# Which heads the two softmax engines take, and twelve exp tiles in flight instead of eight

## The chip, the cores and the metric

The kernel runs on one core of one Trainium2 chip. Time is device time in microseconds. Before the change, four runs gave a median of 1343.49 us (1343.4 to 1343.71). One further look is the profiled execution, whose trace is read below.

A core has a matrix engine (TensorE, in the trace PE, its weight loads apart as PEld), a vector engine (VectorE, DVE), a scalar engine (ScalarE, ACT), a general engine (GpSimd, POOL) and a queue engine (SyncE, SP). Each works through its own list of instructions in order; semaphores tie the lists together.

## The reference

Two kinds of layer alternate, A, B, A, B, on x of shape 2048 x 512 in bf16. Cut to what matters:

```python
def A(x, w_r, w_i):                      # spectral
    X = rfft2(x); X = X * (w_r + 1j * w_i)
    return irfft2(X)

def B(x, wq, wk, wv, wo):                # 32 heads of 16, one shared K and V
    q = (x @ wq) split into heads; k = x @ wk; v = x @ wv
    p = softmax(q k^T / 4); return (p v, heads joined) @ wo

x = x + A(layernorm(x)); x = x + B(layernorm(x))
x = x + A(layernorm(x)); x = x + B(layernorm(x))
```

Both layers A share one filter, both layers B one set of weights.

## The kernel before, in words

**Layers.** A layer pair is A, then B. The spectral transform is done as matmuls with cosine and sine tables along both axes, with small additions and subtractions (radix steps) on DVE between them: a forward part (`add_front`), a middle with the second transform and the filter (`add_middle`), and a way back, layer norm and the K and V projections (`add_back`). Near the end of the filter, `radix_d` (L1177) makes sums and differences of the filtered spectrum with `radix2` (L56), four tiles of 4 x 512 called xd, which the inverse matmuls in `inv` (L1186) read.

**Attention.** There are 32 blocks in a layer: four blocks of 512 query columns, times eight sets of four heads. A block meets 16 chunks of 128 keys. One unit is one head of one block with one chunk: a score matmul (32 contraction rows, 128 keys, 512 queries), an exponential, and a matmul with V (PV) that also sums the denominator. The four heads of a block lie in the four 32-row strips of the matrix array: a score matmul of head h uses strip h, and score matmuls of different strips run side by side. PV matmuls use four 32-column strips, one per head, and are issued in packs of four.

**Two ways to exponentiate.** ACT takes two heads at once: two score matmuls fill one of two double PSUM buffers "sa", one exp (L1318) reads both and writes an SBUF tile "e". DVE takes one head: one score matmul fills one of four PSUM buffers "b"; a first phase (L1325, `p1`) makes the bits of a bf16 power of two by a multiply and an add, and two more phases are this pattern plus a constant, added on 64-bit words by POOL (L1329) or, rarely, by DVE (L1331). PV then reads three phases, with weights that make a smoother approximation.

**The planner.** No order is written by hand. When the program is built, `Plan` keeps an estimated clock per engine and, step by step, issues whichever candidate can start first (`run`, L197). `do_scores` (L478) issues a run of up to five score tiles: the kind (ACT or DVE) whose engine would run dry first. `peek` (L614) says which heads a kind would take next, and `take` (L628) takes them. The four heads of a chunk belong at first to one kind, and an idle kind may take the rest of the other's. ACT takes the first two in order; DVE takes the first one whose strip is not already used in the present run. If a strip repeats in a run, `do_scores` counts another pass. `usable` (L351) refuses another ACT score when as many exp tiles are unread by PV as `E_BUFS` (L131) allows, which is 8. `round` (L416) forms packs of four PV matmuls, and lets smaller ones go when a kind has reached its limit. `fill` (L454) inserts dummy matmuls on zeros where the planner sees too little matmul activity.

Around the attention the same planner issues the work of the neighbouring layers: query projections, output projections (L1366), statistics, the next layer's front part. The result is a fixed list for each engine.

**Buffers.** Thirteen tiles "e" of 128 x 1024 bf16 serve exp tiles and some short-lived tiles (`t2`, L981, takes the one that was freed longest ago; `free2`, L990, gives it back). `wrote` (L993) drops a write-after-write wait when the same engine wrote the buffer before.

Of the kernel before, what the change touches and what calls it, by code (L numbers as in the profile page):

```python
# [8 lines left out]
ACT = mybir.ActivationFunctionType  # L9
ALU = mybir.AluOpType  # L10
P = 128
BF = mybir.dt.bfloat16
# [40 lines left out]
    return tabs  # L53


def radix2(nc, sd, x, piece):  # L56

    nc.vector.tensor_tensor(out=sd[:, 2 * piece:2 * piece + 2, :], in0=x[:, 0:2, :], in1=x[:, 2:4, :],  # L58
                            op=ALU.subtract if piece else ALU.add)


def radix4(nc, sd, x, half, o, piece):
# [53 lines left out]
class Plan:  # L116
# [12 lines left out]
    PORT = True  # L129
    POOL_LAG = 2600.0  # L130
    E_BUFS = 8  # L131
    T_BUFS = 4
    WIN = 3413.0
    WARM = 3500.0
# [17 lines left out]
    def __init__(self):  # L152
        self.t = {"PE": 0.0, "ACT": 0.0, "DVE": 0.0, "POOL": 0.0}
        self.mode = ""
        self.sa = [0.0, 0.0]
        self.bank = [0.0] * self.NB
        self.use = [None] * self.NB
        self.bg = {"PE": [], "ACT": [], "DVE": [], "POOL": []}
        self.n = 0
        self.hist = []  # L160
        self.at = None
        self.act_fifo, self.p1_fifo, self.ph_fifo, self.pool = [], [], [], []
        self.pv = []
        self.half = None
        self.live = {"ACT": 0, "DVE": 0}
        self.bufs = {"ACT": self.E_BUFS, "DVE": self.T_BUFS}
        self.dve_last = ""
        self.acc_of = {}
        self.bg_last = self.port = 0.0
        self.ranks, self.base = None, 0  # L170

    def ranked(self, which):
# [24 lines left out]
    def run(self, goal):  # L197
        while not goal():
            best = None
            for c in (self.pe_next(), self.act_next(), self.dve_next(), self.pool_next()):  # L200
                if c is not None and (best is None or c[0] < best[0]):
                    best = c
            best[1](best[0], *best[2:])


# [210 lines left out]
    def round(self):  # L416
        at = self.at
        avail = []
        free = self.slot_free("b")
        for e in sorted(self.pv, key=lambda e: e[:2]):  # L420
            if (e[2] in self.acc_of or free is not None) and e[4] // 4 in at.v_ready:
                avail.append((max(e[0], at.v_ready[e[4] // 4]),) + e[1:])
        if not avail:
            return None
        b0 = min(e[2] for e in avail)
        t0 = 0.0 if b0 in self.acc_of else free
        heads, sel = set(), []
        for e in avail:
            if e[2] == b0 and e[3] not in heads:
                heads.add(e[3])  # L430
                sel.append((max(e[0], t0),) + e[1:])
        if len(sel) < 4 and b0 + 1 in self.acc_of:
            for e in avail:
                if e[2] == b0 + 1 and e[3] not in heads:
                    heads.add(e[3])
                    sel.append(e)
        full = any(self.live[k] >= self.bufs[k] for k in ("ACT", "DVE"))
        return sel if len(sel) == 4 or self.made(b0) or full else None

    def made(self, b, h=None):  # L440
# [147 lines left out]
class Attn:  # L588
# [25 lines left out]
    def peek(self, kind, strips=()):  # L614


        cur = self.cur[kind]
        if not cur and self.groups:
            b, kc = self.groups[0]
            cur = [(b, kc, h) for h in range(4)]  # L620
        if not cur:
            other = self.cur["DVE" if kind == "ACT" else "ACT"]
            cur = other if kind == "DVE" or len(other) > 1 else []
        if kind == "ACT":
            return cur[:2]
        return sorted(cur, key=lambda u: u[2] in strips)[:1]

    def take(self, kind, us):  # L628
        if not self.cur[kind] and self.groups:
# [48 lines left out]
class Layer:  # L678
# [83 lines left out]

    def add_middle(self):
        p, em = self.plan, self.em
        self.mid, self.fil = [], []
        for u in range(4):
            evs, two = [], u in self.two
# [21 lines left out]
            if u == 3 and not two:  # L789
                a = p.add("DVE", 1733.0, evs[:2], lambda k, u=u: em.filt(self, u, 0, 2), order=10 + u, port=True)  # L790
# [10 lines left out]
    def add_back(self):  # L801
        p, em, at = self.plan, self.em, self.at
        left = [T]
        for t in range(T):
            o = 20 + 10 * t
            cs = []
            for b in range(2):
                es = []
                for j in range(2):
                    if t == 0 and not self.direct:  # L810
# [3 lines left out]
                                  lambda k, t=t, b=b, j=j, m=m: em.inv(self, t, b, j, m.slot, (1,)), order=o)  # L814
                    elif t == 0:
# [3 lines left out]
                                  lambda k, b=b, j=j, m=m: em.inv0(self, b, j, m.slot, 1), order=o)  # L819
# [8 lines left out]
            for j in range(0, R, w):  # L828
                key, ks = ("b", t, j), []
                for i, r in enumerate(range(j, j + w)):  # L830
# [11 lines left out]
                    z = p.add("DVE", 597.0, [y], lambda k, t=t, r=r, y=y: em.add_x(t, r, y.slot), give=(y,), order=o + 1)  # L842
# [15 lines left out]
            def v_got(k, t=t):  # L858
                at.v_ready[t] = k.end + p.LAT[k.eng]
                left[0] -= 1  # L860
                if left[0] == self.EARLY:
                    at.dve_on = True
                    at.dve_from = k.end - 2000.0
# [61 lines left out]
class Emit:  # L925


    def __init__(self, ctx, tc, ins, out):
# [21 lines left out]
        self.part = const.tile([P, 2], F32, name="part")  # L950
        self.wv = const.tile([P, NC, DH], BF, name="wv")
        self.tc = tc
        self.e2 = [const.tile([P, 1024], BF, name=f"e2_{i}") for i in range(13)]
        self.idle, self.home, self.writer = list(range(13)), {}, {}
        self.WO = const.tile([P, 4, D], BF, name="WO")
        self.junk = const.tile([P, 512], BF, name="junk")
        self.eps = const.tile([P, 1], F32, name="eps")
# [197 lines left out]
    def turn(self, L, u, piece):  # L1155
        if piece == 0:
            L.sd_of[("x", u)] = self.t4([4, 512])
        radix2(self.nc, L.sd_of[("x", u)], L.X[u], piece)
        if piece:
            L.X[u] = L.sd_of.pop(("x", u))  # L1160

# [14 lines left out]

    def radix_d(self, L, u, piece):  # L1177
        if piece == 0:
            L.Dz[u] = self.t4([4, 512], tag="xd", bufs=4)
        radix2(self.nc, L.Dz[u], L.X[u], piece)  # L1180

    def load_it(self, L, t):
        L.IT[t] = self.t4([4, 640], tag="it", bufs=2)
# [2 lines left out]
    def inv(self, L, t, b, j, slot, ks):  # L1186
        for v in range(T):
            if v <= t + 1 and v not in L.IT:
                self.load_it(L, v)
        ps = self.ps(slot).rearrange("p (u x) -> p u x", u=2)  # L1190
        for k in ks:
            u = 2 * j + k
            for a in range(2):
                for i in range(2):
                    w = 128 * (3 - (t * a + i) % 4)
                    z = L.Dz[u][:, 2 * (t % 2) + a, 256 * i + 128 * b:256 * i + 128 * b + 128]
                    self.nc.tensor.matmul(ps[:, k, :], lhsT=z, rhs=L.IT[t][:, u, w:w + 256], start=(a == 0 and i == 0),  # L1197
                                          stop=(a == 1 and i == 1), skip_group_check=True)

    def inv0(self, L, b, j, slot, k):  # L1200

# [255 lines left out]
```

The softmax here doesn't subtract the row's maximum and nothing guards it: scores larger than these inputs give would overflow.

## Time and profile before

| what | value |
| --- | --- |
| median of four runs | 1343.49 us |
| profiled execution, its own time | 1343.71 us |
| profiled execution, span | 1341.9 us |
| score matmuls on PE | 4096 (L1313) |
| PV matmuls on PE | 7360: 2464 for exp tiles, 4896 for phases (L1335) |
| exps on ACT | 1232, mean 1094 ns |
| first phases on DVE | 1632, mean 675 ns |
| phase adds on POOL | 815, mean 1049 ns |
| sums and differences into xd on DVE | 16, median 683 ns (L58) |

The span runs from the first to the last instruction of the program. "Busy" is the time in which an engine shows an instruction. An instruction's shown duration can reach over the start of the next one on the same engine, so busy time is more than what the engine needs, and the step from one start to the next says more. A line such as "A <- B: 8.4, 8, 4.0" in the waits view says that A's engine stood idle for 8.4 us in 8 waits, 4.0 at most, until B released it. L numbers are lines of the kernel before.

### The profile page before, as it was taken

To read this page: it belongs to the slowest core of one execution; us is meant where nothing else is said; L and a number is where in the kernel's file an instruction comes from. 1 tells how busy PE (TensorE), PEld (TensorE's weight loads), DVE (VectorE), ACT (ScalarE), POOL (GpSimd) and SP (SyncE) were. 2 spreads that over 40 slices of the span, in tenths; PEclk is the share of its full clock that TensorE was granted. 3 is DMA by queue.
4 is the path that set the end of the run, shared out by engine and by line. 5 is a ranking of instruction groups with operands and counts; after the bars stand their busy time and mean duration, and the time that the engine had idled before them with its cause. 6 is when DMAs were issued, how large, how long until landed. Compare 5 with 4: busy or idle time off the path is not lost. (4 is left out here: it accounts for less than half of the span.)

```text
span 1341.9 us, 31571 instructions
## 1 busy us (share of the span) xinstructions
PE 1305.1 (97%) x12978; PEld 428.4 (32%) x13046; DVE 1291.2 (96%) x2317; ACT 1225.6 (91%) x1390; POOL 848.1 (63%) x831
## 2 busy tenths in 40 slices
PE   9999999999999999999999999999999999999998
PEld 5642223222222232222246422222222222322222
DVE  6998999999999999999969999999999999999998
ACT  6478999999999999899954889999999999998996
POOL 0004777767776777667720068777777777876775
PEclk9999999999999999999999999999999999999999
DMA  9100000010001000100051000000000000000000
GB/s 292 41 1 1 2 1 2 2 33 1 2 2 33 1 2 2 32 2 2 1 165 41 1 2 1 2 2 6 13 2 2 6 13 2 2 1 17 1 1 17
DMA packets 29041, 25.16 MB, mean 19 GB/s; under 512 B 8672, under 2 KB 27616, under 8 KB 28896
## 3 DMA queue, kind: packets, MB, share of 16 engines
q1 hardware_dynamic: 28608, 22.58, 5.8%
q8 instruction: 102, 1.67, 0.5%
q10 hardware_dynamic: 288, 0.56, 0.1%
q14 instruction: 43, 0.35, 0.1%
HBM read 17.89 MB, written 3.67 MB: 16 GB/s over the span
## 5 line engine op out<-in xcount | busy, mean ns | idle before, releaser
L1318 ACT ACTIVATE e<-sa 128x1024 bf16<-128x1024 f32 x1232 | 1142.6, 1094 | 24.6 <-PE sa L1313 20.1
L1329 POOL INT64_ADD w<-w x815 | 845.3, 1049 | 475.4 <-DVE w L1325 425.9
L1325 DVE TENSOR_SCALAR w<-b 128x512 uint16<-128x512 f32 x1632 | 996.1, 675 | 7.5 <-PE sa L1313 3.4
L1335 PE MATMUL b<-w,vs 128*32 128x512 bf16 x4896 | 544.3, 385 | 2.4 <-POOL w L1329 1.1
L1335 PE MATMUL b<-e,vs 128*32 128x512 bf16 x2464 | 411.5, 386 | 1.0 <-DVE w L1325 0.4
L1313 PE MATMUL sa<-w,KA 32*128 32x512 bf16 x1248 | 257.5, 381 | 6.1 <-ACT e L1318 3.8
L1313 PE MATMUL b<-w,KB 32*128 32x512 bf16 x832 | 255.5, 381 | 2.8 <-DVE w L1325 1.7
L1313 PE MATMUL sa<-w,KB 32*128 32x512 bf16 x1216 | 252.5, 381 | 5.6 <-ACT e L1318 2.2
L1335 PEld LDWEIGHTS <-vs 128*32 128x32 bf16 x7360 | 142.6, 94 | 330.7 <-issue 316.1
L1313 PE MATMUL b<-w,KA 32*128 32x512 bf16 x800 | 235.7, 381 | 0.7 <-DVE w L1325 0.2
L1313 PEld LDWEIGHTS <-KB 32*128 32x128 bf16 x2048 | 84.0, 91 | 224.0 <-issue 218.5
L1313 PEld LDWEIGHTS <-KA 32*128 32x128 bf16 x2048 | 82.3, 91 | 226.0 <-issue 217.9
L1342 DVE STREAM_TRANSPOSE raw<-b 128x512 f32<-128x512 f32 x64 | 44.8, 700 | 4.0 <-PE b L1335 4.0
L1028 DVE BATCH_NORM_STATS2 st<-x_sb 128x6 f32<-128x512 bf16 x52 | 35.3, 679 | 4.2 <-DMA x_sb<-in_A_x_dram 3.8
L1248 DVE TENSOR_TENSOR x_sb<-b,x_sb 128x512 bf16<-128x512 f32 x52 | 34.4, 675 | 3.4 <-PE b L1366 2.6
L1297 PE MATMUL b<-gx,wq 128*128 128x512 bf16 x101 | 35.2, 385 | 0.8 <-issue 0.2
L1366 PE MATMUL b<-WO,w 128*128 128x512 bf16 x116 | 34.2, 382 | 1.3 <-DVE w L1325 0.5
L1197 PE MATMUL b<-it,xd 128*128 128x256 bf16 x256 | 30.8, 273 | 3.2 <-DVE xd L58 3.2
L1237 PE MATMUL b<-tab_PS,w 128*128 128x512 bf16 x122 | 31.0, 379 | 0.5 <-issue 0.3
L1099 PE MATMUL b<-tab_PH,e 128*128 128x512 bf16 x118 | 30.5, 380 | 0.9 <-ACT w L1112 0.3
L1257 ACT CAST e<-b 128x512 bf16<-128x512 f32 x28 | 16.0, 587 | 15.4 <-PE b L1197 14.9
L1197 PEld LDWEIGHTS <-xd 128*128 128x128 bf16 x256 | 24.4, 98 | 9.5 <-DVE xd L58 3.9
(84 smaller groups left out, 572.8 us busy)
## 6 DMA issues: line engine op xcount, KB each, us to landing
it<-const_IT SPq DMA_DIRECT2D x8, 640.0 KB, 6.5
w<-const_FT SPq DMA_DIRECT2D x8, 512.0 KB, 7.1
x_sb<-in_A_x_dram SPq DMA_DIRECT2D x4, 512.0 KB, 6.9
w<-in_A_w_r_dram SPq DMA_DIRECT2D x8, 256.0 KB, 6.7
w<-in_A_w_i_dram SPq DMA_DIRECT2D x8, 256.0 KB, 7.1
out_dram<-x_sb SPq DMA_DIRECT2D x16, 128.0 KB, 1.8
way<-x_sb SPq DMA_DIRECT2D x6, 256.0 KB, 2.2
tab_PH<-const_PH ACTq DMA_DIRECT2D x1, 512.0 KB, 5.1
```

The lines of the kernel that those rows point to most:

```text
L1028: self.nc.vector.bn_stats(st, self.ps(slot) if slot else self.x[:, x[1], x[0], :])
L1197: self.nc.tensor.matmul(ps[:, k, :], lhsT=z, rhs=L.IT[t][:, u, w:w + 256], start=(a == 0 and i == 0), stop=(a == 1 and i == 1), skip_group ...
L1237: self.nc.tensor.matmul(self.ps(slot), lhsT=L.UT[t][:, b, r, 128 * i:128 * i + 128], rhs=self.PS[:, s, :], start=(s == 0), stop=(s == n - ...
L1248: self.nc.vector.tensor_tensor(out=x, in0=self.ps(slot), in1=x, op=ALU.add)
L1297: self.nc.tensor.matmul(self.ps(slot), lhsT=self.wq[:, c, g * 128:(g + 1) * 128], rhs=self.xTc(at, qb, c), start=(c == 0), stop=(c == NC - ...
L1313: self.nc.tensor.matmul(o, lhsT=KX[rs, kc * P:(kc + 1) * P], rhs=at.QT[qb][rs, g, :], start=True, stop=True, skip_group_check=True)
L1318: self.wrote("ACT", e, self.nc.scalar.activation(out=e, in_=self.ps(slot), func=ACT.Exp, scale=SCALE))
L1325: self.nc.vector.tensor_scalar(out=t[0][:, j], in0=self.ps(slot), scalar1=P1_SCALE, scalar2=P1_BIAS, op0=ALU.mult, op1=ALU.add)
L1329: self.nc.gpsimd.int64_add(t[p][:, 0:n].bitcast(U64), t[0][:, 0:n].bitcast(U64), DELTA[p] * FOUR)
L1335: self.nc.tensor.matmul(self.ps(slot)[32 * h:32 * h + 32, :], lhsT=V[:, kc, :], rhs=rhs, start=first, stop=last, skip_group_check=True)
L1342: self.nc.vector.transpose(out=at.raw[(qb, g)][:, par].rearrange("p a b -> p (a b)"), in_=self.ps(slot))
L1366: self.nc.tensor.matmul(self.ps(slot), lhsT=at.OT[t][:, g, r * P:(r + 1) * P], rhs=self.WO[:, g, :], start=(g == 0), stop=(g == g1 - 1), s ...
```

## The change

There are four parts.

1. `peek` sorts the heads that a kind may take. Heads whose strip is already used in the present run come last; for DVE this is the old rule, for ACT it is new. Among the rest, when the other kind has one or two heads left of its chunk, the heads in those strips come last.
2. The limit of unread exp tiles is 12 (`E_LATE`) instead of 8 from the moment the last V tile of a layer is ready until `add_middle` plans the next layer. Otherwise it stays 8.
3. The tiles xd are gone. `radix_d` writes the sums and the differences into one "e" tile each, eight in a layer; each is given back after its fourth use in `inv`. There are 21 tiles "e" instead of 13, in place of the four xd tiles, which are twice as large.
4. If nothing can be issued, `run` sets a flag under which `round` lets a smaller pack go, instead of failing.

```diff
-def radix2(nc, sd, x, piece):
+def radix2(nc, o, x, piece):
+    nc.vector.tensor_tensor(out=o, in0=x[:, 0:2, :], in1=x[:, 2:4, :], op=ALU.subtract if piece else ALU.add)
...
     E_BUFS = 8
+    E_LATE = 12
...
+            if best is None:
+                assert not self.force
+                self.force = True
+                continue
+            self.force = False
             best[1](best[0], *best[2:])
...
-        full = any(self.live[k] >= self.bufs[k] for k in ("ACT", "DVE"))
+        full = self.force or any(self.live[k] >= self.bufs[k] for k in ("ACT", "DVE"))
...
+        taken = lambda x: {u[2] for u in self.cur[x]} if 0 < len(self.cur[x]) <= 2 else ()
         if kind == "ACT":
-            return cur[:2]
-        return sorted(cur, key=lambda u: u[2] in strips)[:1]
+            d = taken("DVE")
+            return sorted(cur, key=lambda u: (u[2] in strips, u[2] in d))[:2]
+        a = taken("ACT")
+        return sorted(cur, key=lambda u: (u[2] in strips, u[2] in a))[:1]
...
     def add_middle(self):
+        p.bufs["ACT"] = p.E_BUFS
...
             def v_got(k, t=t):
                 left[0] -= 1
+                if left[0] == 0:
+                    p.bufs["ACT"] = p.E_LATE
...
-        self.e2 = [const.tile([P, 1024], BF, name=f"e2_{i}") for i in range(13)]
+        self.e2 = [const.tile([P, 1024], BF, name=f"e2_{i}") for i in range(21)]
...
     def radix_d(self, L, u, piece):
         if piece == 0:
-            L.Dz[u] = self.t4([4, 512], tag="xd", bufs=4)
-        radix2(self.nc, L.Dz[u], L.X[u], piece)
+            L.Dz[u] = [[self.t2([2, 512]), 4] for _ in range(2)]
+            for z, _ in L.Dz[u]:
+                self.writer.pop(self.home[id(z)][0], None)
+        radix2(self.nc, L.Dz[u][piece][0], L.X[u], piece)
...
     def inv(self, L, t, b, j, slot, ks):
-                    z = L.Dz[u][:, 2 * (t % 2) + a, 256 * i + 128 * b:256 * i + 128 * b + 128]
+                    z = L.Dz[u][t % 2][0][:, a, 256 * i + 128 * b:256 * i + 128 * b + 128]
+            d = L.Dz[u][t % 2]
+            d[1] -= 1
+            if d[1] == 0:
+                self.free2(d[0])
```

More of the change, by code (lines that the diff above doesn't have):

```diff
@@ L53, in host_tables @@
     return tabs
-def radix2(nc, sd, x, piece):
-    nc.vector.tensor_tensor(out=sd[:, 2 * piece:2 * piece + 2, :], in0=x[:, 0:2, :], in1=x[:, 2:4, :],
-                            op=ALU.subtract if piece else ALU.add)
+def radix2(nc, o, x, piece):
+    nc.vector.tensor_tensor(out=o, in0=x[:, 0:2, :], in1=x[:, 2:4, :], op=ALU.subtract if piece else ALU.add)
 def radix4(nc, sd, x, half, o, piece):
@@ L202, in run @@
                     best = c
+            if best is None:
+                assert not self.force
+                self.force = True
+                continue
+            self.force = False
             best[1](best[0], *best[2:])
@@ L952, in __init__ @@
         self.tc = tc
-        self.e2 = [const.tile([P, 1024], BF, name=f"e2_{i}") for i in range(13)]
-        self.idle, self.home, self.writer = list(range(13)), {}, {}
+        self.e2 = [const.tile([P, 1024], BF, name=f"e2_{i}") for i in range(21)]
+        self.idle, self.home, self.writer = list(range(21)), {}, {}
         self.WO = const.tile([P, 4, D], BF, name="WO")
@@ L1157, in turn @@
             L.sd_of[("x", u)] = self.t4([4, 512])
-        radix2(self.nc, L.sd_of[("x", u)], L.X[u], piece)
+        radix2(self.nc, L.sd_of[("x", u)][:, 2 * piece:2 * piece + 2, :], L.X[u], piece)
         if piece:
```

## The prediction

> **What bounds the kernel now.** I read the page first: busy shares, then its chain.
>
> ```profile
> span 1341.9 us, 31571 instructions
> PE 1305.1 (97%) x12978; PEld 428.4 (32%) x13046; DVE 1291.2 (96%) x2317; ACT 1225.6 (91%) x1390; POOL 848.1 (63%) x831
> ...
> PEclk9999999999999999999999999999999999999999
> ...
> ACT e L1318 19%; DVE w L1325 8%; PE b L1335 6%; PE sa L1313 3%; PE b L1313 3%; DVE w L1170 1%; DVE x_sb L1248 1%; DVE st L1028 1%; PE b L1366 1%; DVE raw L1342 0%; PE b L1297 0%; PE b L1197 0%; PE b L1237 0%; PE b L1010 0%; DVE xnt L1052 0%
> ```
>
> Three engines look full, the TensorE clock is full everywhere, and the chain hops between ACT, DVE and PE. DMA queues carry nothing here. So I cut the span where the DVE's first-phase line (L1325) starts and stops in each layer; the columns of this windows view are the length, then busy time and count of PE, PEld, DVE, ACT, POOL.
>
> ```profile
> 111.06:678.72 567.66, 557.12 (x5746) 158.69 (x5766) 562.60 (x962) 556.69 (x611) 418.48 (x410) 1.00 0.04 10
> 678.72:776.47 97.75, 92.02 (x711) 52.48 (x719) 79.95 (x196) 54.87 (x85) 2.48 (x3) 1.00 0.18 55
> 776.47:1331.50 555.03, 545.53 (x5732) 156.18 (x5749) 550.30 (x922) 544.91 (x590) 423.32 (x408) 1.00 0.01 4
> ```
>
> The two attention stages (call them B and D) are 1122.7 of 1341.9 us, and only they are touched. "Busy" flatters ACT: an exp shows 1097 ns, but in the chain view of stage D runs of exps follow each other faster, 106.64/116 = 0.919 us each:
>
> ```profile
> 947.83 42.58 ACT e L1318 x46
> 1104.03 106.64 ACT e L1318 x116
> ```
>
> Start to start, the commonest step is 0.904 us for an exp and 0.598 us for a DVE first phase. Summing, over the records, what each step is longer than that gives the true slack: ACT 23.1 us in B and 22.0 in D (means 0.942 and 0.941), DVE 11.9 and 8.7 (mean 0.606). DVE is the tightest engine, ACT next. Much of ACT's slack is a few holes, in the waits view of B and the same view of D, and the timeline shows the largest:
>
> ```profile
> ACT e L1318 <- PE sa L1313: 8.4, 8, 4.0
> ```
> ```profile
> ACT e L1318 <- PE sa L1313: 8.6, 6, 2.0
> ```
> ```profile
> 551.83 4.69 ACT L1318 ACTIVATE e<-sa 128x1024 bf16<-128x1024 f32 x5
> 560.55 1.94 ACT L1318 ACTIVATE e<-sa 128x1024 bf16<-128x1024 f32 x2 [4.03 <-PE sa L1313]
> ```
>
> In that hole PE runs the output projection (L1366) and hardly any PV matmuls (L1335), so exp tiles stay unread; at eight unread ones the planner may issue no more ACT scores.
>
> PE's score groups, last. A score matmul uses one of four 32-row strips, and a group is the run of score matmuls between other PE work:
>
> ```profile
> 525.94 0.38 PE L1313 MATMUL b<-w,KB 32*128 32x512 bf16 x1
> 525.95 0.60 PE L1313 MATMUL sa<-w,KB 32*128 32x512 bf16 x2
> 526.47 0.39 PE L1335 MATMUL b<-e,vs 128*32 128x512 bf16 x1
> ...
> 528.10 0.39 PE L1313 MATMUL sa<-w,KB 32*128 32x512 bf16 x2
> 528.11 0.39 PE L1313 MATMUL b<-w,KB 32*128 32x512 bf16 x1
> 528.42 0.40 PE L1335 MATMUL b<-w,vs 128*32 128x512 bf16 x3
> ```
>
> Both groups hold three score matmuls. In the first, DVE's head sits in the same strip as one of ACT's pair; the third matmul starts 0.22 us late and PV follows after 0.53 us. In the second all strips differ: 0.32 us. Over all groups the medians are 0.531 to 0.534 and 0.322: a repeated strip costs 0.21 us.
>
> **The change part by part.** The order of every engine is fixed when the program is built, so its counts are known beforehand. SP's order is unchanged, and all engines run the same order up to the start of B.
>
> *Heads in different strips.* Score groups go from 1209 to 1217, those with one repeat from 404 to 234: 170 x 0.211 = 35.9 us less on PE. Dummy matmuls fall by 20 and PV matmuls by 44, together 16 packs of four x 0.226 (median from pack to pack) = 3.6 us. Changes between score, PV and full-array work rise by 17, at 0.321 - 0.226 = 0.095 each: +1.6. PE sheds 37.9 us. It is not the bound, so this is worth what ACT and DVE stop waiting.
>
> A rule speaks against the size of that: the Trainium skill, "TensorE: Matmul & The Clock Gate", Part 3, section "Measured speedup vs the span model", gives four 32-row tiles together 3.07 times, not four times, the throughput of one. By it a full pack would take 1.30 single passes, and as an estimate a merged group would save 0.146 instead of 0.211 us, 24.8 us in all. The trace's quick four-strip groups (tenth percentile) take 0.324 us against 0.321 for three, so I keep the row; the forecast does not hang on it.
>
> *Twelve exp tiles.* In the built order, 57 exps of B and D now fill the eighth tile; afterwards 37 fill a ninth to twelfth. The holes that this can fill are the 8.4 + 8.6 = 17.0 us of waits shown.
>
> *The new split.* ACT's exps rise by 6 in B and 5 in D; DVE's first phases fall by 12 and 10 (an exp does two heads, a first phase one). The POOL adds fall by 12, off the path: POOL waits for DVE 425.9 us in total. DVE: 12 x 0.607 + 10 x 0.606 = 13.3 us less. Two half-size phase adds move onto DVE (L1331's full-size row is 0.694 us; bounds 0 to 0.69 each, taken at half, as half the elements): +0.7. DVE's work falls by 12.6 us.
>
> ACT gains 11 x 0.904 = 9.9 us of work. For the span to follow DVE down by 12.6, ACT's slack has to fall from 45.1 to 22.6, that is by 22.5. The price list allows it narrowly: 17.0 of holes; and the exps whose scores stood in a group with a repeat are 56 ns over the floor, the others 29, so about 177 exps (428 in 411 such groups now, 1.04 per group) x 27 ns = 4.8. Together 21.8.
>
> *Difference tiles in the exp buffers.* The same 16 DVE subtractions and additions at 0.683 us (L58, xd), into two-part tiles. Each takes the oldest freed of 21 buffers. Were one not yet read, DVE would wait for a PV pack: 16 x 0.226 = 3.6 us at worst, nothing at best, since the dedicated xd buffers cause no wait in the trace. I take 0: twenty-one less twelve leaves the buffer long read. The chain through 678.72:776.47 stays; if the cover failed, PE's inverse matmuls (L1197), waiting 3.2 us for L58 now, would wait longer.
>
> *Tail.* The order ends with a first phase without an exp beside it and two phase adds: bounds 0 and 1.3 us; counted above.
>
> **Sum:** DVE -12.6, and ACT allows 21.8 - 9.9 = 11.9. I take the middle, 12.3. The profiled run took 1343.71 us, 1.8 around its span and 0.2 above the median. 1343.5 - 12.3 = 1331.2. Its own range: if DVE's six long steps went as well (over 0.5 us too long each, 4.8 in all), 1326; if a quarter of the 21.8 us stayed, ACT would allow 6.5 us: 1337. If half stayed it would allow 1 us, which is the third rival.
>
> **The rivals.**
>
> *The stalls melt on all three engines.* If PE's 37.9 us were passed on whole: DVE's floor is 12.6 + 20.6 = 33.2 below, ACT's 45.1 - 9.9 = 35.2, so 1310. For: all three engines are interlocked, and PE delays feed both others. Against: in steady stretches most ACT and DVE steps already sit at the floor (757 of 1231 exps within 10 ns), so nothing upstream can shorten them.
>
> *ACT becomes the bound: slower.* If ACT's mean step stays where it is, because its lateness comes from the two score buffers "sa" rather than from strips or tiles, 11 more exps cost 6 x 0.942 + 5 x 0.941 = 10.4 us: 1353.9. For: the chain of stage D is 46% exps, and PE itself waits for exps to free those buffers (6.0 us in all, 25 times). It decides when the mean ACT step stays above 0.932; at 0.921 it supports the forecast. Against: those 25 waits average 0.24 us, and the long holes are not theirs.
>
> *Hidden anyway.* PE's time turns into PE idling, DVE's lost work into DVE waits: 1343.5. For: ACT's account closes only if nearly all its known stalls go. Against: all of DVE's waits on PE that the waits view lists are 3.1 us in B and 2.7 in D now.
>
> **How the numbers follow.** A kernel time tells from no change at about 0.2%, 2.7 us. Chances: forecast 0.65, all stalls melting 0.12, hidden 0.09, ACT bound 0.14. The range holds the forecast, the hidden case, and half of the melting one, to 1317 and 1347; beyond lie 0.06 and 0.14. Faster 0.65 + 0.12 = 0.77, same 0.09, slower 0.14. Likeliest case alone: 1326 to 1337.
>
> **What would show it.** Right: 1243 exps stepping at about 0.92 us, 1610 first phases at 0.606, the ACT wait on "sa" in B and D well below 17.0 us, groups of three scores at 0.32 us, stage B near 560.5 and D near 549.5 us, the stretch between them at 97.7. Wrong: an ACT step of 0.94 with long waits on "sa" (ACT bound); a DVE step above 0.62 (hidden); L58 or L1197 waiting more (buffers); or a granted clock below full, which nothing here foresees.

## The result, and the profile after

The changed kernel takes 1341.06 us (median of 31 runs, 1340.34 to 1345.98); the kernel before takes 1343.59 us beside it (51 runs, 1343.08 to 1344.17). The medians differ by 2.5 us, or 0.2%; the ratio taken over all the runs is 0.9986 (1.9 us), with a 95% interval of 0.9981 to 0.9991. The forecast was 12.3 us. The value lies inside the range of 1317 to 1347 us, but near the rival "hidden anyway" (1343.5), not near the forecast (1331.2).

The profiled execution of the kernel after took 1344.4 us, and its TensorE clock was lowered for some 10 us near the end; 12 of 32 executions show a mean clock of 0.995 to 0.998 and take 1341.65 to 1345.98 us, while 18 of the others take 1340.34 to 1341.22, about 1340.6 in the middle (the last two, at 0.999, take 1342.1 and 1342.6). So by an estimate, 1344.4 - 1340.6, about 3.8 us of the profiled time belong to that stretch, and they lie in stage D.

The page of the kernel after: the span, the engines, the clock in 40 slices, and the chain that ended last by engine and by line.

```profile
span 1342.6 us, 31412 instructions
PE 1301.9 (97%) x12913; PEld 439.0 (33%) x12982; DVE 1282.1 (95%) x2297; ACT 1231.7 (92%) x1401; POOL 834.9 (62%) x819
...
PEclk9999999999999999999999999999999999999989
...
ACT 49%; PE 31%; DVE 16%; issue 2%; DMA 1%; SPq 1%; DVEq 0%
...
L1336 ACT ACTIVATE e<-sa 128x1024 bf16<-128x1024 f32 x1243 | 1149.5, 1121 | 18.0 <-PE sa L1331 13.2
...
L1343 DVE TENSOR_SCALAR w<-b 128x512 uint16<-128x512 f32 x1610 | 984.5, 676 | 15.8 <-PE b L1331 9.3
```

The counts are those of the built order: 1243 exps and 1610 first phases. The line of the first phase is now L1343, that of the exp L1336, and the score matmul is L1331. DVE shows 9.1 us less busy time, and the span did not follow it down. The chain's shares can't be compared with those of the page before: there the chain is followed back only to 702 us, and its shares sum to 48%, against 100% here. Followed through stage D alone, exps hold 46.0% of it before and 55.9% after. In the last group, first phases now wait 9.3 us for single-head scores.

The windows view cuts the span at the same places as before: stage B, the stretch between, stage D, and then three slices of 10 us from the end of D. The columns are the window, its length, busy time and count of PE, PEld, DVE, ACT and POOL, the granted clock, DMA share and GB/s.

```profile
110.80:675.53 564.73, 552.88 (x5719) 165.01 (x5741) 555.31 (x949) 560.64 (x618) 412.26 (x404) 1.00 0.04 10
675.53:772.91 97.38, 91.04 (x697) 51.96 (x702) 81.55 (x196) 53.39 (x83) 1.45 (x2) 1.00 0.17 54
772.91:1331.43 558.52, 547.40 (x5697) 160.98 (x5717) 545.46 (x912) 548.55 (x595) 417.23 (x403) 0.99 0.01 4
...
1280.00:1290.00 10.00, 9.96 (x112) 2.93 (x109) 10.00 (x18) 10.00 (x12) 8.59 (x10) 1.00 0.01 2
1290.00:1300.00 10.00, 9.40 (x68) 2.31 (x67) 7.64 (x14) 6.49 (x7) 5.12 (x6) 0.79 0.01 2
1300.00:1310.00 10.00, 10.00 (x92) 2.18 (x92) 7.91 (x14) 7.73 (x8) 6.15 (x6) 0.70 0.00 0
```

B is 2.94 us shorter than before (567.66), where 7.2 were expected. D is 3.49 us longer than before (555.03); without the 3.8 us of the lowered clock it would be about 554.7, so by this estimate it gained next to nothing. The stretch between them, which contains the difference tiles, is 97.38 us, near the expected 97.7.

Steps from start to start, summed over what each is longer than its commonest value, show where the time stayed. One step needs care: the last of a stage, which leads into the next stage. Where ACT's list goes on from B, the timeline shows, before and after:

```profile
683.93 1.01 ACT L1153 CAST w<-sa 128x1024 bf16<-128x1024 f32 x1 [3.73 <-PE sa L1146]
```
```profile
680.50 1.01 ACT L1165 CAST w<-sa 128x1024 bf16<-128x1024 f32 x1 [5.28 <-PE sa L1158]
```

The exps that these waits follow start at 679.17 and 674.18 us, the first behind the end of B (678.72), the second ahead of it (675.53). A sum over all steps that start in B therefore leaves the wait out before and takes it in after. Without the last step of each stage, ACT's slack was 23.0 us in B and 22.0 in D, and it is now 11.6 and 20.9. It fell by 12.6 us, where 22.5 were needed. DVE's slack, counted in the same way, was 9.2 and 8.6 (the 11.9 of the prediction holds 2.7 us of the step that leaves B); it is now 15.0 and 16.6. So the 12.6 us of work that DVE no longer does came back whole as waiting, 13.9 us (4.0 of it between 1288 and 1304.5 us, around the lowered clock).

The waits view of the whole run (who waited for whom, us in all, times, longest), one line of before and then after:

```profile
DVE w L1325 <- PE b L1313: 2.4, 7, 0.5
```
```profile
ACT e L1336 <- PE sa L1331: 13.2, 16, 2.6
...
DVE w L1343 <- PE b L1331: 9.3, 22, 1.0
...
PE sa L1331 <- ACT e L1336: 7.7, 31, 0.5
```

ACT's holes on "sa" in B and D are 2.8 and 7.2 us, where they were 8.4 and 8.6. This is 7.0 us less; the other 5.6 us that ACT's slack lost lie outside the holes. DVE's waits on "b" went the other way, from 2.4 us in the whole run to 9.3. More than half of D's 7.2 us lie in the window from 1288 to 1306 us:

```profile
ACT e L1336 <- PE sa L1331: 4.1, 4, 2.2
```

The trace has the lowered clock from 1295.76 to 1306.00 us. The longest of these waits, 2.2 us, ended at 1292.89, so the lowered clock did not make it; the other three, 1.9 us together, lie inside.

Last, PE. Groups of scores that need two passes became fewer: 234 instead of 404. But the time in all score groups, from a group's first score to PE's next work, went from 529.4 us only to 524.3. The quick groups are as priced: without a repeat, the median is 324 ns (322 before). But more of them are slow: the upper quartile is 379 ns (325 before), and the mean 376 (353). Over the 977 groups without a repeat this is 22 us, and the 234 groups of two passes grew from 595 to 636 ns in the mean, 10 us together. So most of the 35.9 us that the merged passes were to save went into longer groups. The timeline of PE shows a group without a repeat that is slow all the same; the columns are start, shown duration, instruction.

```profile
880.23 0.40 PE L1353 MATMUL b<-e,vs 128*32 128x512 bf16 x4
880.56 0.38 PE L1331 MATMUL b<-w,KA 32*128 32x512 bf16 x1
880.82 0.39 PE L1331 MATMUL sa<-w,KB 32*128 32x512 bf16 x2
881.14 0.40 PE L1353 MATMUL b<-w,vs 128*32 128x512 bf16 x4
```

DVE's head starts at 880.56 and ACT's pair 0.26 us later, although all three strips differ. The pair waits for its PSUM buffer "sa". The trace shows it for nearly all such pairs: of the 631 pairs that follow another score of their group, 377 start more than 0.03 us after it, and 374 of these start 0.04 to 0.06 us after the end of the exp that empties their buffer. Before, 276 of 507 were late, 270 of them in this way. The largest delays, 0.25 to 0.29 us, became more frequent: 73 pairs instead of 28. Groups without a repeat that begin with DVE's head, go on with ACT's pair and are followed by PV are now 329 (160 of three scores, 169 of four; before 47 and 62), and their means are 383 and 410 ns. So a merged pass saves its full 0.21 us only when the buffer is free at that moment.

### The profile page after: what moved, and what is told of

Same layout as the page of the kernel before. It is cut to its first block, busy times and chain, and to the rows that moved or that the text cites. A ratio compares the mean times of both kernels' runs of the same rounds, so it can differ in the third digit from the quotient of the medians.

```text
span 1342.6 us, 31412 instructions
## 1 busy us (share of the span) xinstructions
PE 1301.9 (97%) x12913; PEld 439.0 (33%) x12982; DVE 1282.1 (95%) x2297; ACT 1231.7 (92%) x1401; POOL 834.9 (62%) x819
## 4 chain that ended last, share of the span: by engine, by line
ACT 49%; PE 31%; DVE 16%; issue 2%; DMA 1%; SPq 1%; DVEq 0%
ACT e L1336 49%; PE b L1353 11%; DVE w L1343 8%; PE b L1331 6%; PE sa L1331 6%; PE b L1384 2%; DVE w L1182 1%; PE b L1111 1%; PE b L1255 1%; DVE st L1040 1%; PE b L1315 1%; PE b L1211 1%; DVE x_sb L1266 1%; DVE e L58 1%; DMA w<-const_FT 1%
## 5 line engine op out<-in xcount | busy, mean ns | idle before, releaser
L1336 ACT ACTIVATE e<-sa 128x1024 bf16<-128x1024 f32 x1243 | 1149.5, 1121 | 18.0 <-PE sa L1331 13.2
L1347 POOL INT64_ADD w<-w x803 | 832.0, 1048 | 487.9 <-DVE w L1343 448.1
L1343 DVE TENSOR_SCALAR w<-b 128x512 uint16<-128x512 f32 x1610 | 984.5, 676 | 15.8 <-PE b L1331 9.3
L1353 PE MATMUL b<-e,vs 128*32 128x512 bf16 x2486 | 427.6, 387 | 1.1 <-DVE raw L1360 0.5
L1331 PE MATMUL sa<-w,KA 32*128 32x512 bf16 x1264 | 247.9, 384 | 6.2 <-ACT e L1336 3.9
L1331 PE MATMUL b<-w,KB 32*128 32x512 bf16 x826 | 249.7, 382 | 2.8 <-DVE w L1343 1.5
L1331 PE MATMUL sa<-w,KB 32*128 32x512 bf16 x1222 | 242.4, 381 | 6.1 <-ACT e L1336 3.7
L1331 PE MATMUL b<-w,KA 32*128 32x512 bf16 x784 | 240.3, 384 | 1.3 <-ACT w L1124 0.2
L1331 PEld LDWEIGHTS <-KB 32*128 32x128 bf16 x2048 | 89.1, 91 | 229.2 <-issue 221.8
L1331 PEld LDWEIGHTS <-KA 32*128 32x128 bf16 x2048 | 83.4, 91 | 231.1 <-issue 221.7
L1211 PE MATMUL b<-it,e 128*128 128x256 bf16 x256 | 30.8, 273 | 3.1 <-DVE e L58 3.1
L1111 PE MATMUL b<-tab_PH,e 128*128 128x512 bf16 x118 | 31.6, 381 | 0.8 <-ACT w L1124 0.3
L1211 PEld LDWEIGHTS <-e 128*128 128x128 bf16 x256 | 24.4, 98 | 9.4 <-DVE e L58 3.8
```

The source lines that it names most:

```text
L1111: self.nc.tensor.matmul(self.ps(slot), lhsT=xt[:, cc, P * i:P * i + P], rhs=self.PH[:, cc, :], start=(cc == 0), stop=(cc == NC - 1), skip_ ...
L1331: self.nc.tensor.matmul(o, lhsT=KX[rs, kc * P:(kc + 1) * P], rhs=at.QT[qb][rs, g, :], start=True, stop=True, skip_group_check=True)
L1336: self.wrote("ACT", e, self.nc.scalar.activation(out=e, in_=self.ps(slot), func=ACT.Exp, scale=SCALE))
L1343: self.nc.vector.tensor_scalar(out=t[0][:, j], in0=self.ps(slot), scalar1=P1_SCALE, scalar2=P1_BIAS, op0=ALU.mult, op1=ALU.add)
L1347: self.nc.gpsimd.int64_add(t[p][:, 0:n].bitcast(U64), t[0][:, 0:n].bitcast(U64), DELTA[p] * FOUR)
L1353: self.nc.tensor.matmul(self.ps(slot)[32 * h:32 * h + 32, :], lhsT=V[:, kc, :], rhs=rhs, start=first, stop=last, skip_group_check=True)
```

## Experiments

Two readings stood against each other at first. One: the parts do what was forecast, but some part takes the gain away (the shared tiles, the strips, or the twelve exp tiles). The other: DVE is not the bound, and time taken from it returns as waits. A third was added when the parts alone did not add up: the time of an order depends on chance details of the order, and the kernel before has a lucky one.

### The parts alone

The tiles alone: the kernel after with the old `peek` and the old limit.

```diff
-    E_LATE = 12
+    E_LATE = 8
...
-            d = taken("DVE")
-            return sorted(cur, key=lambda u: (u[2] in strips, u[2] in d))[:2]
-        a = taken("ACT")
-        return sorted(cur, key=lambda u: (u[2] in strips, u[2] in a))[:1]
+            return cur[:2]
+        return sorted(cur, key=lambda u: u[2] in strips)[:1]
```

> Only the tiles: sums and differences go into the e tiles, 21 of them, but the head choice and the limit of eight are as before. Every engine's list has the same instructions in the same order as the kernel before. If sharing the buffers costs nothing, as predicted: 1343.6 within 0.7 us. If DVE waits for unread e tiles at the 16 sums and differences: up to 3.6 us more, 1347.2, all of it between the two attention stages.

It took 1343.64 us, ratio 1.0 (0.9991 to 1.001). Its first two windows and the group of the subtractions and additions (times of one: least, median, most in ns):

```profile
111.06:678.72 567.66, 557.15 (x5746) 158.69 (x5766) 562.60 (x962) 556.71 (x611) 419.26 (x410) 1.00 0.04 10
678.72:776.47 97.75, 92.02 (x711) 52.44 (x719) 79.95 (x196) 54.88 (x85) 2.48 (x3) 1.00 0.18 55
```
```profile
L58 DVE TENSOR_TENSOR e<-w x16: 681/684/691, 43.7 to 721.0; 128x1024 bf16<-128x1024 bf16 x16
```

Both windows have the lengths of the kernel before, 567.66 and 97.75 us, and the operation takes 684 ns where it took 683. The buffers cost nothing.

The strips alone: the kernel after with `E_LATE = 8`.

> The tiles and the head choice, with the limit left at eight. Groups with a repeated strip fall from 404 to 244 (the full change: 234), exps rise by 3 instead of 11. Theory 1 (DVE's work sets the span): DVE loses 6 first phases, 3.6 us, so 1340. Theory 2 (the strips' saving on PE is what arrives, and the limit of twelve gives its share back as new holes): faster than the full change, 1338 or less. Theory 3 (PE's saving comes back as waits of PE for the score buffers): 1341 to 1344.

It took 1346.35 us, ratio 1.0022 (1.0012 to 1.0032): slower than any of the three theories had it, although two-pass groups fell from 404 to 244. ACT's holes on "sa" stayed, at 8.2 and 9.7 us.

The twelve exp tiles alone: the kernel after with the old `peek`.

> The tiles and the limit of twelve, with the old head choice. Groups with a repeated strip stay at 388 + 16 with more than one, exps rise by 9. Theory 1 (DVE's work sets the span): 18 first phases less are 10.9 us, 1333. Theory 2 (the limit moves ACT's holes to later and frees nothing): 1342 to 1346. ACT's waits for PE at the sa buffers tell: 17.0 us in the two attention stages before; under 10 by theory 1, about the same by theory 2.

It took 1335.63 us, ratio 0.994 (0.9926 to 0.9955). Its windows, and ACT's holes in its B and D:

```profile
111.03:677.84 566.81, 558.69 (x5714) 160.27 (x5736) 552.32 (x948) 563.38 (x619) 412.71 (x403) 1.00 0.04 9
...
775.10:1322.53 547.43, 539.29 (x5699) 155.03 (x5719) 545.86 (x918) 545.85 (x591) 421.61 (x406) 1.00 0.01 4
```
```profile
ACT e L1333 <- PE sa L1328: 1.5, 4, 0.8
```
```profile
ACT e L1333 <- PE sa L1328: 0.8, 1, 0.8
```

As theory 1 has it, the holes are filled, 17.0 us to 2.3. D is 7.6 us shorter, while B gained only 0.9. One half of the change alone is faster by 5.4 us than the whole change, and the other half alone is slower than nothing. Either the strips harm, or such differences are between single orders and not between rules.

### How much of an engine's time is on the path

Each of these keeps the built order of the kernel before and adds small work to one engine, evenly spread. The code shown leaves out the scratch tiles and, in the second and third, the line that counts. The first was a memset on DVE after every eighth first phase:

```diff
+        self.n_pad += 1
+        if self.n_pad % 8 == 0:
+            self.nc.vector.memset(self.pad, 0.0)
```

> The kernel before with a memset of a scratch tile (128 x 64) on DVE after every eighth first phase, 204 of them; all other work and the order of the rest are unchanged. An estimate from the smallest DVE rows is 0.07 to 0.1 us each, 14 to 20 us together. If DVE is the tightest engine, as predicted: the span grows by that sum less at most the 20.6 us of DVE slack it can use, that is by at least half, 7 us or more. If ACT sets the pace and DVE has room: under 4 us.

It took 1344.76 us, ratio 1.0009 (0.9999 to 1.0019), against 1343.6 beside it, and settles little, since the load was hardly one. The memsets are there, 112 ns each:

```profile
L1331 DVE MEMSET pad<- x204: 112/112/112, 116.0 to 1332.5; 128x64 f32 x102
```

But the first phase after a memset starts only 0.030 us after it, and the step behind that is 0.545 us instead of 0.598, so one costs DVE 0.021 us net, 4.3 us in all, of which 1.2 us arrived. The next two loads are of a kind whose price could be measured in place, as what they add to the step around them; the third, on PE, is priced by the repeated strip, 0.21 us:

```diff
+        if self.n_pad % 24 == 0:
+            self.nc.vector.tensor_scalar(out=self.pad, in0=self.ps(slot)[:, 0:128], scalar1=P1_SCALE, scalar2=P1_BIAS, op0=ALU.mult, op1=ALU.add)
```

> The kernel before with more work on DVE: after every twenty-fourth first phase, 68 in all, the same operation again on 128 of the 512 columns, into a scratch tile. An estimate is a quarter of the 0.598 us plus some fixed part, 0.17 to 0.25 us each, 12 to 17 us together. If DVE is the tightest engine, as predicted, the span grows by at least half of what DVE gains. If ACT or PE sets the pace, by less than a quarter.

```diff
+        if self.n_pad % 20 == 0:
+            self.nc.scalar.activation(out=self.pad_a, in_=self.ps(slot)[:, 0, 0:128], func=ACT.Exp, scale=SCALE)
```

> The kernel before with more work on ACT: after every twentieth exp, 61 in all, an exp of 128 of the 1024 columns into a scratch tile. An estimate is an eighth of the 0.904 us plus some fixed part, 0.2 to 0.3 us each, 12 to 18 us together. If DVE is the tightest engine: ACT has 45.1 us of slack, so the span grows by less than a quarter of the load. If ACT sets the pace: by at least half.

```diff
+            if j == len(us) - 1:
+                self.n_pad += 1
+                if self.n_pad % 46 == 0:
+                    self.nc.tensor.matmul(o, lhsT=KX[rs, kc * P:(kc + 1) * P], rhs=at.QT[qb][rs, g, :], start=True, stop=True, skip_group_check=True)
```

> The kernel before with more work on PE: after every forty-sixth set of score matmuls, 62 in all, the last one is done again into the same place, which costs as much as a repeated strip, 0.21 us, 13.0 us together. If DVE or ACT is the tightest engine: less than a quarter of it, 3 us. If PE's backlog is what makes the other two late: at least half, 6.5 us.

The rows of the added operations in the kernels with DVE's and with ACT's load:

```profile
L1331 DVE TENSOR_SCALAR pad<-b 128x128 uint16<-128x128 f32 x68 | 18.9, 278 | 0.0
```
```profile
L1324 ACT ACTIVATE pad_a<-sa 128x128 bf16<-128x128 f32 x61 | 21.9, 358 | 0.0
```

| load | by its steps | time, ratio | arrives |
| --- | --- | --- | --- |
| DVE, 68 short first phases | 68 x 0.198 = 13.5 us | 1354.29, 1.0077 (1.006 to 1.0093) | 10.4 us, 77% |
| ACT, 61 short exps | 61 x 0.158 = 9.6 us | 1350.49, 1.0049 (1.0034 to 1.0064) | 6.6 us, 69% |
| PE, 62 repeated scores | 62 x 0.21 = 13.0 us | 1349.88, 1.0045 (1.003 to 1.006) | 6.0 us, 46% |

The kernel before took 1343.9 us beside them. The rank is the prediction's, DVE before ACT before PE, but it is not firm. The distances are small, and PE's price is not one of this run: its score groups grew by only 8.7 us in all, and of these 6.0 us are 69%. The added operations on DVE and ACT also read the PSUM buffer that PE is to fill next, so a part of what arrives may come by way of PE. Still, the shares sum to nearly two, and ACT's is over the half that its expectation set for an engine that sets the pace. No engine alone sets the time: the three are interlocked, and each is on the path for much of the two stages. Work taken from one of them therefore need not come off the time unless the others give way too.

### Neighbouring orders

The planner decides by estimated durations. Changing one of them by a nanosecond changes no instruction's work, only which candidate it picks, and so the order and, by a few heads, the split. Three such nudges of the kernel before:

```diff
-    DVE_P1 = 600.0
+    DVE_P1 = 601.0
```

> The kernel before with one of the planner's assumed durations, DVE's first phase, at 601 instead of 600 ns. Nothing else differs; the planner's greedy choices give another order of the same kind: 594 + 590 exps as before, groups with one repeated strip 413 instead of 404. If the time follows from the counts and the rules, it stays within 1.5 us of 1343.6. If the particular order matters by itself, it moves by more, and differences of that size between the parts of the change say little.

```diff
-    ACT_EXP = 908.0
+    ACT_EXP = 907.0
```

> The kernel before with the planner's assumed exp at 907 instead of 908 ns. Theory A (the order that the kernel before happens to have is a lucky one among its like): slower than 1343.6 by 2 us or more, as the first nudge was by 7. Theory B (nudges scatter to both sides): within 4 us to either side, with no sign to expect.

`HOLD` is the longest time that the planner puts off a run of scores in favour of other work:

```diff
-    HOLD = 200.0
+    HOLD = 190.0
```

> The kernel before with the planner's HOLD at 190 instead of 200 ns. Three exps fewer (594 + 587) by the built order, so 6 first phases more on DVE. Theory A (the kernel before has a lucky order): slower than 1343.6 by 2 us or more. Theory B (scatter to both sides): within 4 us to either side.

They took 1351.21, 1349.37 and 1356.55 us, ratios 1.0055 (1.0034 to 1.0075), 1.0043 (1.0023 to 1.0062) and 1.0094 (1.0065 to 1.0123): all three slower, as the theory of a lucky order says. So a change of 1 ns in one assumption moves the time by more than the studied change does. The same nudges of the kernel after:

> The changed kernel with the planner's assumed exp at 907 instead of 908 ns. If the change is worth what the counts say and the small result is an unlucky order: 1331 to 1338. If the result is what the rules give on the chip, whatever the order: 1338 to 1344.

> The changed kernel with the planner's assumed first phase at 601 instead of 600 ns; 599 + 598 exps against 600 + 595. To be compared with the same nudge of the kernel before, which took 1351.2. If the change is worth 12 us between orders of equal luck: 1339 or less. If it is worth the 2.5 us that the pair of kernels shows: 1346 to 1351.

> The changed kernel with HOLD at 190 instead of 200 ns (the kernel before with this nudge: 1356.6). If the change is worth about 9 us or more between orders of equal luck, as the mean of three pairs says (2.5, 8.5 and 16.4): 1348 or less. If only the pair of un-nudged kernels tells the truth: 1354 or more.

They took 1340.87, 1334.85 and 1339.09 us, ratios 0.9979 (0.9967 to 0.999), 0.9933 (0.991 to 0.9955) and 0.9965 (0.995 to 0.9981). The first lies where its expectation puts a result that does not hang on an unlucky order, so nothing says that the order of the kernel after is an unlucky one; it is the kernel before that stands out. The one with `DVE_P1 = 601` is the fastest of all the kernels here. Its windows:

```profile
110.95:675.23 564.28, 554.54 (x5744) 166.90 (x5743) 557.70 (x952) 559.11 (x617) 414.11 (x405) 1.00 0.04 10
...
772.34:1321.66 549.32, 538.63 (x5688) 162.20 (x5685) 541.75 (x905) 548.65 (x597) 414.87 (x400) 1.00 0.02 4
```

Its D is 549.32 us, where the prediction expected 549.5, though of another order. Then the two halves with the two small nudges, in the order strips with `ACT_EXP`, strips with `DVE_P1`, twelve with `ACT_EXP`, twelve with `DVE_P1`:

> Only tiles and head choice, assumed exp 907 ns (the kernel before with this nudge: 1349.4; the changed kernel: 1340.9). If the head choice is worth nothing or harms, as the un-nudged pair says (1346.4 against 1343.6): 1349 or more. If it is worth most of the full change between orders of equal luck: 1345 or less.

> Only tiles and head choice, assumed first phase 601 ns (the kernel before with this nudge: 1351.2; the changed kernel: 1334.9). If the head choice harms: 1351 or more. If it is worth half of the full change: about 1343.

> Only tiles and the limit of twelve, assumed exp 907 ns (the kernel before: 1349.4; the changed kernel: 1340.9). If the limit alone is the whole gain, as the un-nudged runs say (1335.6 against 1341.1): 1341 or less. If the un-nudged 1335.6 was a lucky order: 1343 to 1348.

> Only tiles and the limit of twelve, assumed first phase 601 ns (the kernel before: 1351.2; the changed kernel: 1334.9). If the limit alone is the whole gain: 1335 or less. If its un-nudged 1335.6 was a lucky order: 1340 to 1347.

All medians in us:

| kernel | no nudge | `ACT_EXP` 907 | `DVE_P1` 601 | `HOLD` 190 | mean of the first three |
| --- | --- | --- | --- | --- | --- |
| before | 1343.6 | 1349.4 | 1351.2 | 1356.6 | 1348.1 |
| strips alone | 1346.4 | 1345.3 | 1346.2 | | 1346.0 |
| twelve alone | 1335.6 | 1345.3 | 1344.5 | | 1341.8 |
| both (after) | 1341.1 | 1340.9 | 1334.9 | 1339.1 | 1339.0 |
| after minus before | -2.5 | -8.5 | -16.4 | -17.5 | -9.1 |

The 5.4 us by which twelve alone beat the whole change turn round under both nudges, to 4.4 and 9.6 the other way, and the 2.8 us by which strips alone were slower turn to 4.0 and 5.0 faster. Both runs of twelve alone lie where their expectations put a lucky first order. So the first three runs told single orders apart, not the parts. Over three orders each, strips give -2.1, twelve -6.3, both -9.1 us, which is about their sum; with three values that differ by up to 10 us, the -2.1 can't be told from nothing. Over the four pairs, the change gives -11.2 us on average, with a standard error of 3.5 (the four differences spread by 7.0).

The traces agree. ACT's holes on "sa" in the whole run, in the three nudged kernels before (the order of the runs above) and in the first two nudged kernels after:

```profile
ACT e L1318 <- PE sa L1313: 24.7, 23, 5.0
```
```profile
ACT e L1318 <- PE sa L1313: 26.0, 23, 4.0
```
```profile
ACT e L1318 <- PE sa L1313: 30.5, 27, 4.0
```
```profile
ACT e L1336 <- PE sa L1331: 12.6, 10, 3.3
```
```profile
ACT e L1336 <- PE sa L1331: 7.0, 10, 2.8
```

In B and D together they are 17.0, 21.7, 22.9 and 27.5 us in the four orders before (none, `DVE_P1`, `ACT_EXP`, `HOLD`), on average 22.3, and 10.0, 9.5, 4.0 and 12.5 in the four after (none, `ACT_EXP`, `DVE_P1`, `HOLD`), on average 9.0. Without the last step of each stage, ACT's slack averages 50.5 us in the four before (45.1, 47.8, 48.4 and 60.5, the last with half clock for 3.4 us of its trace) and 29.9 after (32.5, 29.4, 24.7 and 33.2), in the order of the table. DVE's averages 24.2 (17.8, 26.0, 24.0 and 29.0) and 26.0 (31.6, 27.8, 21.3 and 23.3). So from order to order ACT loses about 20 us of slack and DVE's hardly changes; but the kernel before, as it stood, had the least of both among its four, and the kernel after the most of DVE's. By chance alone, the kernel before would be the best of four once in four. Its constants may also have been chosen because this order measured well; no run here tells the two apart.

Last, the load on PE again, on the kernel after, with the same edit as on the kernel before:

> The changed kernel with the same added work on PE as before: after every forty-sixth set of score matmuls, the last one again, 62 in all, 13.0 us. The kernel before grew by 6.0 us. If the strips freed PE, so that it has room now: under 3 us, 1344 or less. If PE's saving went into waits inside the score groups, and its lateness still counts as before: about 6 us, 1347.

It took 1346.24 us, ratio 1.0024 (1.001 to 1.0037) to the kernel before. Against the kernel after, 5.2 us arrive of 13.0, and 4.3 among executions at full clock; before the change 6.0 arrived. This lies between the two expectations. So PE is not much less on the path than it was, although its list holds 170 fewer second passes.

## Why the prediction was wrong, point by point

- *The counts and the steps of the operations* held: 1243 exps, 1610 first phases, 684 ns for L58, 324 ns for a quick group without a repeat. One reading was too strong: the DMA queues do not carry nothing, their share is 0.04 in B and 0.01 in D; nothing hangs on it.
- *Difference tiles at nothing, and the middle stretch as it was*: right. The tiles alone gave ratio 1.0, and both stretches kept their lengths.
- *"The price list allows it narrowly"* is the step that failed. ACT's slack had to fall by 22.5 us. The term that was too large is the holes: they were to give all of 17.0 us and gave 7.0, most of it in B; D's went from 8.6 only to 7.2. Exps in groups with a repeat were to give 4.8; outside the holes ACT's slack went from 28.1 to 22.5, by 5.6, so that term was about right. Together that is 12.6 of 21.8, against 9.9 us of added exps, and by the prediction's own sum ACT then allows 2.7 us. The measured 2.5 agree with that closer than the sum deserves: in the profiled execution, with its lowered clock, B and D together are not shorter at all.
- *DVE's slack taken over unchanged* failed with it. Without the last step of each stage it rose from 17.8 to 31.6 us, and DVE's mean step from 0.603 and 0.605 to 0.611 and 0.616, against the 0.606 forecast. This has the form of "hidden anyway", though it does not pass the 0.62 that was named as its sign. The reason given against that rival, DVE's waits on PE in D of 2.7 us, left out a line of the same view, 2.1 us of `x_sb` (L1248) on L1366. Part of the mechanism can be seen: first phases wait longer for "b" (2.4 to 9.3 us), and score groups without a repeat now more often begin with DVE's head and wait for ACT's buffers in the middle. That the second brings about the first is not shown.
- *"PE sheds 37.9 us"* was counted rightly and is mis-sized as a time. Score groups as a whole became 5.1 us shorter in the kernel as it stands, 22.4 in its fastest neighbour (507.0 us), where 35.9 were priced. The prediction said that this was worth only what ACT and DVE stop waiting; that holds, but it priced 0.21 us for each merged pass, and a pass whose "sa" buffer is still being read gives less. The reason that was weighed against the row, the Trainium skill, "TensorE: Matmul & The Clock Gate", Part 3, "Measured speedup vs the span model" (four 32-row tiles together 3.07 times the throughput of one), is not what took it: undisturbed groups of three and four scores in the trace after take 321 and 325 ns (tenth percentile), as quick as before (321 and 324).
- *"DVE is the tightest engine, ACT next"*: as a rank not contradicted, though not firm; as a guide wrong. 77%, 69% and 46% of a load arrive; the sum treated DVE as the bound and ACT as a limit, where all three are on the path by turns.
- *"ACT becomes the bound"* was priced at 1353.9, from a mean step that stays at 0.941 or so. The steps are 0.922 in B and 0.938 in D. The latter is above the 0.932 at which it was to decide, but 6.4 us of D's slack lie between 1288 and 1304.5 us, around the lowered clock; without these eleven steps the mean is 0.928, and the time is not above that of before. Its mechanism is partly there: where ACT's pair is late, it starts 0.04 to 0.06 us after the exp that empties its buffer, and the share of exps in the chain of stage D went from 46.0 to 55.9%.
- *What no step had*: the baseline. The prediction read the waits of one order and subtracted what the change removes from them. The runs of neighbours show that an order's waits vary by some 10 us under a nudge that changes no instruction's work, and that the kernel before stood at the low end of its own spread. The pair under study sets the fastest of four orders before against the slowest, by 0.2 us, of four after. Over four pairs of neighbours the change gives -11.2 us, next to the -12.3 forecast, with about 20 us less slack on ACT (the sum had 21.8) and 1.8 us more on DVE (the sum had 0). So the direction and the rough size of the mechanism are borne out by the mean, and a good part of the miss is a matter of which two orders were compared. That the two sizes agree so well may itself be luck, with a standard error of 3.5.
- *A granted clock below full*, named as unforeseen, did occur, for about 10 us in a part of the executions. It costs the median under 0.5 us.

It stays open why the order of the kernel before is better than its neighbours (chance, or constants chosen by measurement), and which decision of the planner lets holes return in the order after; the runs show that it is so for these nudges, not which instruction does it.

## What to carry to other kernels

Where a program orders the work by greedy choices, one pair of orders does not measure a rule: nudge an assumption that changes no work, build three or four neighbours of both versions, and compare the means; then keep the fastest order (here the change with `DVE_P1 = 601`, 1334.85 us). Before a saving on one engine is booked, add a small known load to each engine and see how much arrives; where the shares sum to more than one, the engines are interlocked, and no engine's work can be booked alone. A median price of a merged pass holds only where its buffers are free, so price the whole group's distribution, with its waits. And when waits of a stage are summed, cut the stage in the same place in both runs: one step at its end was 5.4 us of ACT's slack here.

## What the runs showed of the hardware

- The TensorE clock stood at half for 10.24 us in the profiled execution, in windows in which PE was busy 9.40 and 10.00 of 10 us, with 10 of 10 us shown on ACT and DVE in the window before. The Trainium skill, "TensorE: Matmul & The Clock Gate", "HAM oscillation — how this bites in real kernels", puts a lowered clock down to idle gaps of TensorE over about 3.4 us. No gap of that length is in this trace: the longest between a matmul's shown end and the next one's start is 1.6 us. The change removed 20 dummy matmuls, but these are not needed for it: one of four executions of the kernel before with DVE's load, which has them all, took 1356.46 us where the others took 1353.92 to 1354.38, and its trace has half clock for 6.83 us. What sets it off stays open.

```profile
517.00:527.00 10.00, 9.82 (x80) 2.10 (x77) 8.55 (x14) 7.20 (x8) 5.06 (x5) 0.66 0.01 2
```

- A small memset behind a PSUM-reading operation on DVE cost 0.021 us net, though it shows 0.112: the step behind it shrank from 0.598 to 0.545 us.
- In the trace after, a score matmul that waited for an exp's buffer started 0.052 us (median) after the exp's shown end, and the next exp on that buffer 0.51 to 0.68 us later (tenth percentile and upper quartile). From exp to exp on such a buffer pass 1.807 us in the median and 1.826 us at the ninetieth percentile, next to 1.81 for two steps of 0.904. So most pairs that come late in this way cost ACT next to nothing; what they lengthen is the score group on PE.
